# Another order of loads, and of everything behind them, in a fused attention and gating kernel

## The chip, the cores and the metric

The kernel runs on one core of a Trainium2 chip. The time is that of one execution on the device in microseconds (us), and less is better. Three runs of the kernel before gave 409.8, 411.2 and 410.75 us, with a median of 410.75 us.

## The reference, cut to what matters

There are 8 batches of 576 tokens, with 8 heads of 64 columns and 32 memory slots for each head. All data are float32.

```python
# for each batch and head
a   = softmax(phi, over the tokens)               # 576 x 32
k_m = a.T @ k ;  v_m = a.T @ v                    # 32 x 64 each
x   = softmax(q @ k_m.T / 8, over the slots) @ v_m   # the heads side by side: 576 x 512
# for each batch
h    = relu(x @ w_in)                             # 576 x 1024
u, v = h[:, :512], h[:, 512:]
v    = (v - mean(v)) / sqrt(var(v) + 1e-6)        # over the 512 columns
out  = (u * (w_spatial @ v + b_spatial)) @ w_out  # w_spatial is 576 x 576
```

## The kernel before, in words

The program is one long list of steps, written out by hand. Every kind of work is a generator; a letter in a list runs that generator up to its next `yield`, which is usually one instruction group on one engine. The three lists are `START` (lines 26 to 38: the weights, batch 0 and the beginnings of batches 1 and 2), `PLAN` (lines 40 to 47: repeated for batches 1 to 6) and `LAST` (lines 49 to 53: the end of batch 7). A digit after a letter picks a piece of the work (a block of tokens, of columns or of weights), each `'` means one batch ahead, and `*2` means twice. Each engine carries out its own instructions in the order in which the lists emit them, so a list fixes the queue of every engine, the load queue of SyncE (SP) among them. An instruction at the head of a queue that waits holds up everything behind it.

The letters that the texts below speak of are these.

- `P` (`memory_weights`, line 304) loads phi of a batch into the one buffer `phi_sb`, takes the softmax over tokens there, and sums it (`es`). The next phi can only be loaded when the `kvm` products have read the buffer.
- `K` (`memories`, line 337) loads k and then v into the one buffer `kv_sb`; the products `kvm` (line 351) need both; `den`, `kmn` and `vmn` divide by the sums, `tk` and `tv` turn them, and `kT` and `vT` are the copies of that.
- `Q` (`queries`) loads q. For batch 0 it is turned on TensorE (`tq`, copied to `qT_all` on ScalarE); for later batches it comes in pieces of 128 bytes and VectorE turns it (`qT`, line 445).
- `S` (`scores`, and `scores_first` for batch 0) multiplies q with the memories (`sc`), takes the softmax over slots (`rmx`, `sm`, `rsum`) and leaves it turned, as a high and a low part (`ah` and `al`).
- `D1` and `D0` (`load_win`) load the right and the left half of the columns of w_in, four pieces of 512 KB each. `E0` and `E1` decode the right half from the first and the last two pieces, `L0` and `L1` the left one. A decode has four instructions: ScalarE line 196, VectorE line 198 (the sign), ScalarE line 202, VectorE line 204 (the result, in `win_sb`).
- `M1` and `M0` (`products`) multiply the memories with the right and the left half of w_in (`mp`), again split into `mh` and `ml`.
- `V` (`gate`, five blocks of tokens: `pv`, the statistics `st` and `mv`, then `vh` and `vl`, for the last block the tile `t`) and `U` (`units`, four blocks of columns: `pu`, `u`) are the two halves of h.
- `W` (`load_spatial`) loads w_spatial (`w_sb`, 1152 KB, and `w_rem`) and the bias; `T0` to `T4` turn it on TensorE (`wt`) and split it into `wth` and `wtl`, and `B` puts the bias beside it.
- `G` (`spatial`, `ps`, `g`, `gh`, `gl`) multiplies with w_spatial and gates, `X` loads and decodes w_out, and `O` (`project`, `po`, `o`) multiplies with it and stores.
- `Z` (`warm_up`, line 798) is a product whose result nobody reads.

The low part of a split comes from one of two engines (`low`, line 156). If the name of the tile stands in `ON_VECTOR`, VectorE subtracts the high part (line 177). If it doesn't, TensorE subtracts it with one or two products (line 165) and ScalarE copies the rest (line 175). Names are `wtl` with the block, and `ml` with batch, half and part.

PSUM has two tags. `b1` has four buffers of one bank and `b2` has two buffers of two banks. The tiles of `T`, `U` and `G` and the scores are in `b2`, so a third of them waits until one of the two before it has been read for the last time.

In `START` before, SP loads in this order: phi, q, k and v of batch 0, the four pieces of `D1`, the first piece of `D0`, phi of batch 1, w_spatial, the rest of `D0`, k of batch 1, the first half of its q, its v, and the second half of its q.

Of the kernel before, what the change touches and what calls it, by code (L numbers as in the profile page):

```python
# [23 lines left out]


START = """
    P Q P Z P K*2 D1 P Q P*2 Q*2 P*2 Q P*3 Q P Z P Q D1 Q K E0 D1*2 P*2 K*2 Z K*2 E0 K Q*2 K E1
    K*2 E0 Q D0 E1*2 K P' E0 Z S P'*2 S W S P' S Z S D0 Z P' T0 T2 S T0 P' S*2 D0 E1 T0 T2 D0 P'
    S*2 P' S B S M1 P' L0 T0 T2 T1 M1 T2 S L1 S P' M1 S M1 L0 M1 S L1 S*4 T3 K' M1 S T1 L1 S Q' M1
    Z L0 L1 V2 L0 V2 V0 K' T1 P' V2 M0 P'*2 V0 M0 P' K' M0 P' V2 V0*2 M0 T1 K' M0 T4 Q' X1 T3 V1  # L30
    M0 V2 V0 M0 U2 K' V2 T3 U2 P'' V1 X1 T4 T3 V3 V0 U1 Q'*2 K' V1 X0 T4 X0 S U2 U1 K' T4 V1 K' U3
    K'*2 B U3 V2 V1 U1 V0 V1 U0*2 Q'*2 P'' V1 V3 K' X1 V3 U3 P'' V4 P'' V3 U0 X1 K' S' V4 S'*2 X0
    K'' M1' Q'' M0' M1' G0 S'*2 M1' V3 V4 K'' V3 G1 S' M1' G1 V4 P'' G1 V4 M0' G0 M0' V3 P'' G0
    V4*2 X0 P'' V4 G1 X1 P'' X0 S' G1 M0' X0 X1 G0 X0 M1' G3 G0 X0 M1' X1 P'' G3 X1 G1 G3 M0' G1
    G3 G0 G2 G1 G0 G2 P'' M0' G0 Q'' G1 M0' G0 G2*2 G3 O2 G2 O3 S' G2 S' G3 G2 P'' G3 O1 S' O3
    S'*2 O2 G2 S' O2 O3 S' P'' S' P'' O1 O0*2 O1 S' G2 P'' O1 S' G3 M1' G3 U2' S'*2 O3 O0*2 P''
    V1' Q'' O2 V1'*2 Q'' V1'
"""

PLAN = """  # L40
    K' V4 V0 U2 V1 P'' U0 V4 Q' U0 Q'' K' U1 K' Q' U1 V0 P'' V2 U3*2 V0 V3 V0 V2 K' U3 K' S' U1 S'
    K' M1' M0' V2 S'*2 V3 M1' V2 V3*2 V4 G0 V2 G1 S' V3 G0 S' M1' V3 V2 V4 V3 G1 V4 G1 S' M0'
    P''*2 M0' G1 S' G0*2 G3 G1 M1' M0' P'' Q'' G3 G0 G1 P'' S' G3 M0' M1' G1 G3 P'' M1' P'' M0'
    K'' S' G1 M1' G2*2 G0 G2 G1 G0 S' G0 O3 S' P'' G2 G0 O1 G3 G2 G3 S' G2 G3 G2 S'*2 O0 M0' S' O1
    U2' P'' O0 O3 O1 G3 P'' S'*2 P'' S' O0 O3 P''*2 O3 K''*2 V1' K'' O1 V4' V1' G3 V1' V4' O2*2
    V4' O0 V1' O2 P''' G2 V0'*2 G2 O4 Q'' V1' U2' O4 U0' V0' O4 V1' V2' K''' Q'' O2 O4 K''
"""

LAST = """
    U2 V0 V2 V0 V4 V0 U0 V1 U3 U0 U3 V3 V2 U1 V0 U3 V4 U1 V3 V2 G0 V4 U1 V2*2 V4 V3 G0 G1*2 V3 V2  # L50
    V3 V4 G1 G0 V3*2 G0*2 G1 G3 G0 G1 G3 G1 G2 G3 G2 G0 G2 G1*2 O2 G1 G2 O0 G2 G3 G2 V1 G2 G0 G2*2
    G3*3 O1*3 G3 O2 O0 O2 G0 O4 O1 G3 O4 O0 O4 O0 O4 O3*3 O2 O3
"""

FINAL = int(LAST.split()[-1][1])

ON_VECTOR = set(
    """
    E0 E1 L0 L1 X0 X0.sign X1 X1.sign ml000 ml001 ml010 ml101 ml110 ml111 wtl3 wtl4
""".split()  # L60
)

# [816 lines left out]
```

## Time and profile before

| what | value |
|---|---|
| median of three runs | 410.75 us |
| time of the profiled execution | 410.63 us |
| its span, from the first to the last instruction | 408.8 us |
| TensorE busy with products | 392.5 us (96%) |
| VectorE, ScalarE, GpSimd busy | 287.9, 229.9, 47.6 us |
| mean granted clock of TensorE | 0.994 of full |
| moved by the DMA engines | 50.7 MB |

In the rows further down PE is TensorE, DVE is VectorE, ACT is ScalarE and SPq is the queue of SyncE. A row of a timeline begins with its start and its length in us. Where the engine had been idle before it, the idle time and what ended it stand in brackets. Rows with `x2` hold two instructions in a row.

### The profile page before, as it was taken

The page shows a single profiled execution, that of the slowest core. Times are in us where ns is not written, and L with a number is a line of the kernel's source. Part 1 is how long each engine was busy: PE and PEld are TensorE (multiplying, and loading weights), DVE is VectorE, ACT ScalarE, POOL GpSimd, SP SyncE. Part 2 cuts the span into 40 slices and gives each one's busy share as a digit, 9 for nine tenths or more (in the row PEclk, how much of TensorE's full clock was granted, in tenths as well). Part 3 has the DMA queues.
Part 4 walks back from the last instruction along what each step waited for, and adds up shares of the span by engine and source line. Part 5 has one row for each costly group of instructions (what it writes and reads, how often), then busy time and mean ns, then how long its engine had stood idle before and what let it go on. Part 6 is the DMA issues. An engine that isn't in the chain of part 4 may idle for free.

```text
span 408.8 us, 9476 instructions
## 1 busy us (share of the span) xinstructions
PE 392.5 (96%) x3961; PEld 335.0 (82%) x3961; DVE 287.9 (70%) x543; ACT 229.9 (56%) x423; POOL 47.6 (12%) x131
## 2 busy tenths in 40 slices
PE   4788999999999999999999999999999999999996
PEld 2544779889898879989798879989798879989984
DVE  1589999986896469947796469947796559843430
ACT  2669888538634477247634477238635477148321
POOL 1000311002200310002200311002200311014000
PEclk9989999999999999999999999999999999999999
DMA  8999997023911683046801683045800210020003
GB/s 308 392 371 225 253 249 171 2 104 83 259 66 58 223 140 120 0 134 184 195 2 49 230 139 120 0 140 174 199 2 26 80 28 0 2 77 27 0 22 108
DMA packets 85790, 50.70 MB, mean 124 GB/s; under 512 B 66226, under 2 KB 70322, under 8 KB 85748
## 3 DMA queue, kind: packets, MB, share of 16 engines
q1 hardware_dynamic: 85748, 50.10, 43.0%
q8 instruction: 31, 0.51, 0.5%
q14 instruction: 11, 0.09, 0.1%
HBM read 40.65 MB, written 9.44 MB: 123 GB/s over the span
## 4 chain that ended last, share of the span: by engine, by line
PE 88%; DMA 5%; DVE 4%; ACT 1%; issue 1%; SPq 0%; ACTq 0%
PE ps L734 29%; PE po L774 24%; PE pu L696 12%; PE pv L630 10%; PE kvm L351 4%; PE mp L598 3%; DMA kv_sb<-in_v_dram 3%; DMA w_sb<-in_moe_w_spatial_dram 2%; PE sc L532 2%; PE pv L639 1%; PE pv L640 1%; ACT raw L202 1%; PE wt L264 0%; DVE ml L177 0%; PE tk L391 0%
## 5 line engine op out<-in xcount | busy, mean ns | idle before, releaser
L734 PE MATMUL ps<-wth,vh 128*128 128x288 f32 x256 | 56.3, 301 | 0.0
L734 PE MATMUL ps<-wth,vl 128*128 128x288 f32 x256 | 54.8, 295 | 0.0
L734 PE MATMUL ps<-wtl,vh 128*128 128x288 f32 x256 | 54.5, 294 | 0.0
L756 ACT CAST gh<-g 128x512 fp32r<-128x512 f32 x32 | 19.7, 620 | 56.2 <-DVE g L745 55.9
L774 PE MATMUL po<-woh,gl 128*128 128x512 f32 x128 | 50.4, 393 | 0.0
L774 PE MATMUL po<-woh,gh 128*128 128x512 f32 x128 | 50.2, 392 | 0.0
L774 PE MATMUL po<-wol,gh 128*128 128x512 f32 x128 | 50.2, 392 | 0.0
L659 POOL TENSOR_SCALAR rs<-mv 128x1 f32<-128x1 f32 (+1 forms) x40 | 9.2, 229 | 322.1 <-DVE mv L656 313.6
L734 PEld LDWEIGHTS ps<-wth,vh 128*128 128x128 f32 x256 | 41.1, 188 | 6.6 <-PE mp L598 5.9
L654 DVE BATCH_NORM_STATS2 st<-vr 128x6 f32<-128x512 f32 (+1 forms) x40 | 27.3, 683 | 21.8 <-ACT vr L635 16.9
L734 PEld LDWEIGHTS ps<-wth,vl 128*128 128x128 f32 x256 | 41.1, 188 | 0.0
L734 PEld LDWEIGHTS ps<-wtl,vh 128*128 128x128 f32 x256 | 41.0, 188 | 0.0
L784 ACT COPY o<-po 128x512 f32<-128x512 f32 x35 | 20.4, 587 | 34.0 <-PE po L774 34.0
L674 DVE TENSOR_TENSOR vl<-vr,vh 128x512 fp32r<-128x512 f32 x32 | 21.9, 687 | 24.1 <-ACT vh L672 24.0
L669 ACT ACTIVATE vr<-vr,sh,rs 128x512 f32<-128x512 f32 (+1 forms) x40 | 32.7, 816 | 0.3 <-POOL sh L664 0.2
L635 ACT ACTIVATE vr<-pv 128x512 f32<-128x512 f32 x32 | 19.2, 600 | 23.2 <-PE pv L630 23.0
L745 DVE TENSOR_TENSOR g<-u,ps 128x576 f32<-128x576 f32 x32 | 23.9, 749 | 10.5 <-PE ps L734 10.5
L774 PEld LDWEIGHTS po<-woh,gh 128*128 128x128 f32 x128 | 24.0, 188 | 5.6 <-ACT vr L635 1.2
L774 PEld LDWEIGHTS po<-woh,gl 128*128 128x128 f32 x128 | 24.0, 188 | 5.3
L696 PE MATMUL pu<-ah,mh 128*128 128x288 f32 x128 | 27.8, 299 | 0.5 <-DVE qT L445 0.5
L774 PEld LDWEIGHTS po<-wol,gh 128*128 128x128 f32 x128 | 24.1, 188 | 4.4
L696 PE MATMUL pu<-al,mh 128*128 128x288 f32 x128 | 27.5, 296 | 0.0
(143 smaller groups left out, 855.0 us busy)
## 6 DMA issues: line engine op xcount, KB each, us to landing
kv_sb<-in_k_dram SPq DMA_DIRECT2D x8, 1152.0 KB, 8.2
kv_sb<-in_v_dram SPq DMA_DIRECT2D x8, 1152.0 KB, 8.1
out_dram<-o SPq DMA_DIRECT2D x32, 256.0 KB, 2.7
q_sb<-in_q_dram SPq DMA_DIRECT2D x28, 288.0 KB, 4.8
phi_sb<-in_phi_dram SPq DMA_DIRECT2D x8, 576.0 KB, 5.2
raw<-in_moe_w_in_dram SPq DMA_DIRECT2D x8, 512.0 KB, 11.4
raw<-in_moe_w_out_dram SPq DMA_DIRECT2D x4, 512.0 KB, 6.6
q_all<-in_q_dram SPq DMA_DIRECT2D x1, 1152.0 KB, 6.5
```

The source lines that it names most:

```text
L351: nc.tensor.matmul(kvm[r][32 * j : 32 * j + 32], phi_sb[halves[r], j, i, :], kv_sb[halves[r], j, :, i * D : (i + 1) * D], start=(i == 0), ...
L630: nc.tensor.matmul(pv, x[:, r, cs], m[:, r, DM:DFF], start=(n == 0), stop=(n == 5))
L635: nc.scalar.activation(vr, pv, AF.Relu)
L654: nc.vector.bn_stats(st6, vr)
L669: nc.scalar.activation(vr, vr, AF.Identity, bias=sh, scale=rs)
L674: nc.vector.tensor_tensor(vl[:, st, :], vr, vh[:, st, :].bitcast(F32), op=ALU.subtract)
L696: nc.tensor.matmul(pu[:, hf, 0:HALF], m[:, r, cs], a[:, r, hf * HALF : (hf + 1) * HALF], start=(n == 0), stop=(n == 5),)
L734: nc.tensor.matmul(ps[:, hf, 0:HALF], a, w[:, hf * HALF : (hf + 1) * HALF], start=(n == 0), stop=(n == len(ops) - 1),)
L745: nc.vector.tensor_tensor(g.rearrange("p (a s) -> p a s", a=2), u[:, dt, :].rearrange("p (a s) -> p a s", a=2), ps[:, :, 0:HALF], op=ALU.mult,
L756: nc.scalar.copy(hi, x)
L774: nc.tensor.matmul(po, a, w, start=(n == 0), stop=(n == 11))
L784: nc.scalar.copy(o, po)
```

## The change

Only the three lists and the set `ON_VECTOR` change. The generators are the same, and every step of them still runs. SP's new order at the start is: phi and q of batch 0, the first piece of `D1`, k, the second piece of `D1`, v, the last two pieces of `D1`, w_spatial and the bias, phi of batch 1, the four pieces of `D0`, the first half of q of batch 1, its k, its v, and the second half of its q. On ScalarE the first instructions of both decodes `E0` and `E1` stand ahead of `kmn`, and there is one product `Z` less. `wtl1` and `ml100` move to VectorE, and `ml010` and `ml111` leave it. The order of all other work, in the batches behind as in the first, is new.

```diff
--- before.py
+++ after.py
@@ -24,39 +24,38 @@
 
 
 START = """
-    P Q P Z P K*2 D1 P Q P*2 Q*2 P*2 Q P*3 Q P Z P Q D1 Q K E0 D1*2 P*2 K*2 Z K*2 E0 K Q*2 K E1
-    K*2 E0 Q D0 E1*2 K P' E0 Z S P'*2 S W S P' S Z S D0 Z P' T0 T2 S T0 P' S*2 D0 E1 T0 T2 D0 P'
-    S*2 P' S B S M1 P' L0 T0 T2 T1 M1 T2 S L1 S P' M1 S M1 L0 M1 S L1 S*4 T3 K' M1 S T1 L1 S Q' M1
-    Z L0 L1 V2 L0 V2 V0 K' T1 P' V2 M0 P'*2 V0 M0 P' K' M0 P' V2 V0*2 M0 T1 K' M0 T4 Q' X1 T3 V1
-    M0 V2 V0 M0 U2 K' V2 T3 U2 P'' V1 X1 T4 T3 V3 V0 U1 Q'*2 K' V1 X0 T4 X0 S U2 U1 K' T4 V1 K' U3
-    K'*2 B U3 V2 V1 U1 V0 V1 U0*2 Q'*2 P'' V1 V3 K' X1 V3 U3 P'' V4 P'' V3 U0 X1 K' S' V4 S'*2 X0
-    K'' M1' Q'' M0' M1' G0 S'*2 M1' V3 V4 K'' V3 G1 S' M1' G1 V4 P'' G1 V4 M0' G0 M0' V3 P'' G0
-    V4*2 X0 P'' V4 G1 X1 P'' X0 S' G1 M0' X0 X1 G0 X0 M1' G3 G0 X0 M1' X1 P'' G3 X1 G1 G3 M0' G1
-    G3 G0 G2 G1 G0 G2 P'' M0' G0 Q'' G1 M0' G0 G2*2 G3 O2 G2 O3 S' G2 S' G3 G2 P'' G3 O1 S' O3
-    S'*2 O2 G2 S' O2 O3 S' P'' S' P'' O1 O0*2 O1 S' G2 P'' O1 S' G3 M1' G3 U2' S'*2 O3 O0*2 P''
-    V1' Q'' O2 V1'*2 Q'' V1'
+    P*4 Q Z P*2 Q D1 Q K P*3 Q D1 P*2 Q P*2 Q*3 K P*2 Q K D1 E0 D1 K E1 K Z Q K*5 W K E1 S E1 Q P'
+    S T0 E0 T0 E1 K S D0 S E0 D0 B S*2 T0 D0 P' S Z D0 S T2 Q' E0 T0 T2 L0 P' Z S P' M1 K' S K' T2
+    P' Z S M1 T2 P' Q' P' T3 S M1 L1 L0 P' S M1 S P' M1 S P' T3 S T1 S*4 M1 S M1 Z S L1 P' V0 P' B
+    T1 L1 V2 L0 L1 T3 L0 V0 K' P' M0 T1*2 V2 P' V0 P' K' M0 T4 M0 V2 X1 M0 V0 V1 M0 K' T4 T3 X1 V2
+    K'*2 T4 M0 V0 M0 V2 P'' X0 V1 K' T4 U0 Q' U0 U1*2 K' V2 Q' K' V1 K'' X1 U0 V3 V2 U2 V0 U2 U1
+    U3 Q' S V1 V3 V1 K' X1 P'' V0 V3 U3 V4 K' Q' V3 P'' S' V1 M1' M0' U2 G0 U3 X0 P'' V1 P'' Q''
+    V4 S'*2 M1' V3 V4 G0 X0 V4 X1 V4 V3 S'*2 V4 G1 P'' M0' M1' V4 G1 M1' S' M0' X0 K'' P''*2 G0 V3
+    V4 X0 G1 G0 X1 M1' G0 G1 M1' G2 X0 G1 M0' X1 X0 S' G0 G1 G2 P''*2 X0 G3 X1 G3*2 G0 G2 G1 G3 G2
+    G1 O2 O3 G0 S' G1 G0 M1' G2*2 G3 M0' G3 G2 S' M0' P'' G3 S' O1 O2 O3 O1 S' Q'' O0 O2 S'*3 P''
+    S' O3 O0 S' O3 G2 S' G3 O2 S'*2 O1 G3 V1' G2 O0 P'' V1' M0' P''*2 O0 O1
 """
 
 PLAN = """
-    K' V4 V0 U2 V1 P'' U0 V4 Q' U0 Q'' K' U1 K' Q' U1 V0 P'' V2 U3*2 V0 V3 V0 V2 K' U3 K' S' U1 S'
-    K' M1' M0' V2 S'*2 V3 M1' V2 V3*2 V4 G0 V2 G1 S' V3 G0 S' M1' V3 V2 V4 V3 G1 V4 G1 S' M0'
-    P''*2 M0' G1 S' G0*2 G3 G1 M1' M0' P'' Q'' G3 G0 G1 P'' S' G3 M0' M1' G1 G3 P'' M1' P'' M0'
-    K'' S' G1 M1' G2*2 G0 G2 G1 G0 S' G0 O3 S' P'' G2 G0 O1 G3 G2 G3 S' G2 G3 G2 S'*2 O0 M0' S' O1
-    U2' P'' O0 O3 O1 G3 P'' S'*2 P'' S' O0 O3 P''*2 O3 K''*2 V1' K'' O1 V4' V1' G3 V1' V4' O2*2
-    V4' O0 V1' O2 P''' G2 V0'*2 G2 O4 Q'' V1' U2' O4 U0' V0' O4 V1' V2' K''' Q'' O2 O4 K''
+    U0 V1 Q' K' V0 U2 V4 V1 K' V0*2 P'' V2 Q' V0 U3 U1*2 V3 P'' K' V2*2 K' U3 U1 V4 S' P'' S' K'
+    S' V3 S' V4 V2 V3 S' M1' V4*2 V2 M0' S' G0*2 M0' V3 M1' V3 P'' V3 V2 V3 G1*2 S' G0 M1' G1 S'
+    G0 G1 P'' M1' G0 M1' G2 G0 G2 M0' G1 P''*2 S' G3 G0 P'' G2 G1 G0 S' P'' S' G1 M1' G3*3 G1 M1'
+    G2 O1 G1 G0 G3 G2 S' G2 G3 S' G2 S' G3 P'' O0 S' M0' S' O1 M0' O0 O1 G3 P'' U0' U2' P'' O3 M0'
+    G2 S' O0 O3 P'' G2 S' M0' P'' K''*2 G3 O4 S' O3 V0' Q'' O4 V1' V4' O2 O1 V0' Q'' K'' U2' P'''
+    O3 O2 O4 O0 U0' Q''' V1' Q'' K'' K''' V1'*2 O4 V4' V1' V0' K''' V2' V4' O2*2 K'' U3'
 """
 
 LAST = """
-    U2 V0 V2 V0 V4 V0 U0 V1 U3 U0 U3 V3 V2 U1 V0 U3 V4 U1 V3 V2 G0 V4 U1 V2*2 V4 V3 G0 G1*2 V3 V2
-    V3 V4 G1 G0 V3*2 G0*2 G1 G3 G0 G1 G3 G1 G2 G3 G2 G0 G2 G1*2 O2 G1 G2 O0 G2 G3 G2 V1 G2 G0 G2*2
-    G3*3 O1*3 G3 O2 O0 O2 G0 O4 O1 G3 O4 O0 O4 O0 O4 O3*3 O2 O3
+    V1 V0 U0 V3 V0 V2 U2 U3 V0 V4 V1 V4 U1 V2 V0 V3 U3 V4 U1 V2 V3*2 V2 U1 V2 G1 V4 V3 G1 G0 V2 G0
+    V3 V4 G0 V3 G1*3 G0 G1 G0 G2*3 G0*2 G1 G2 G1 G3 G0*2 G3 O1 G2 G3*2 G1 G3 O4 G3 G2 G3 O3 G3 G2
+    G3 O3 G2 O3 G2 O2 U3 O0 U0 O3 O1 O4 O2 O0 O1 O4 O1 O2 O4 O2 O0*2
 """
 
 FINAL = int(LAST.split()[-1][1])
 
 ON_VECTOR = set(
     """
-    E0 E1 L0 L1 X0 X0.sign X1 X1.sign ml000 ml001 ml010 ml101 ml110 ml111 wtl3 wtl4
+    E0 E1 L0 L1 X0 X0.sign X1 X1.sign ml000 ml001 ml100 ml101 ml110 wtl1 wtl3 wtl4
 """.split()
 )
 
```

## Rows read from the trace of the kernel before

**Rows 1.** The page, DMA share in 40 slices of the span, in tenths.
```profile
DMA  8999997023911683046801683045800210020003
```

**Rows 2.** Waits of PE, whole run: who waited for whom, us, times, longest.
```profile
PE wt L264 <- DMA w_sb<-in_moe_w_spatial_dram: 1.4, 1, 1.4
...
PE pu L696 <- DVE qT L445: 0.5, 1, 0.5
```

**Rows 3.** Busy time by engine, 30 to 80 us; then clock and DMA.
```profile
30.00:80.00 50.00, 47.72 (x505) 38.50 (x490) 48.16 (x77) 41.23 (x67) 6.61 (x16) 0.98 0.76 189
```

**Rows 4.** Timeline of SP's queue, the load of w_spatial.
```profile
16.59 0.51 SPq L248 DMA_DIRECT2D w_sb<-in_moe_w_spatial_dram  x1
```

**Rows 5.** Timeline of ACT, 16 to 20 us.
```profile
16.24 1.12 ACT L196 ACTIVATE raw<-raw 128x1024 int32<-128x1024 uint32 x1 [2.92 <-DMA raw<-in_moe_w_in_dram]
17.27 0.61 ACT L378 ACTIVATE kmn<-kvm,den 128x128 f32<-128x128 f32 x2
...
18.77 1.14 ACT L196 ACTIVATE raw<-raw 128x1024 int32<-128x1024 uint32 x1
19.82 0.35 ACT L400 COPY kT<-tk 128x256 f32<-128x256 f32 x1
```

**Rows 6.** Timeline of PE, 13 to 61 us.
```profile
13.84 2.22 PE L351 MATMUL kvm<-kv_sb,phi_sb 64*32 64x128 f32 x143 [1.21 <-DMA kv_sb<-in_v_dram]
...
21.16 2.07 PE L463 MATMUL sc<-kT,qT_all 64*64 64x32 f32 x116 [0.28 <-issue]
...
41.67 0.43 PE L165 MATMUL wt<-wth,minus 128*128 128x256 f32 x2
42.03 1.09 PE L598 MATMUL mp<-win_sb,vT 64*32 64x512 f32 x16
42.91 2.21 PE L351 MATMUL kvm<-kv_sb,phi_sb 64*32 64x128 f32 x143
...
45.13 1.09 PE L264 MATMUL wt<-ident,w_sb 128*128 128x128 f32 x8
...
48.57 0.42 PE L696 MATMUL pu<-ah,mh 128*128 128x288 f32 x2 [0.50 <-DVE qT L445]
...
60.52 0.54 PE L734 MATMUL ps<-wth,vh 128*128 128x288 f32 x2
```

**Rows 7.** Timeline of DVE, 22 to 66 us.
```profile
22.73 0.69 DVE L295 TENSOR_TENSOR half<-phi_sb 128x512 f32<-128x512 f32 x1 [0.21 <-DMA phi_sb<-in_phi_dram]
...
23.79 0.82 DVE L477 TENSOR_REDUCE rmx_all<-sc 128x20 f32<-128x640 f32 x1
...
29.04 0.29 DVE L317 TENSOR_REDUCE cm<-mt 128x2 f32<-128x128 f32 x1 [0.84 <-PE mt L314]
...
33.94 0.69 DVE L177 TENSOR_TENSOR ml<-mp,mh 128x512 fp32r<-128x512 f32 x1
...
36.43 1.22 DVE L198 SCALAR_TENSOR_TENSOR raw<-raw 128x1024 int32<-128x1024 int32 x1
37.56 1.65 DVE L514 TENSOR_TENSOR al<-ta,ah 128x384 fp32r<-128x384 f32 x2
39.12 2.50 DVE L204 SCALAR_TENSOR_TENSOR win_sb<-raw 128x1024 int32<-128x1024 int32 x2
...
46.38 0.74 DVE L177 TENSOR_TENSOR wtl<-wt,wth 128x576 fp32r<-128x576 f32 x1
...
50.42 0.76 DVE L287 TENSOR_TENSOR ws<-b_sb,ws 1x576 fp32r<-1x576 f32 x1
...
58.39 0.68 DVE L650 TENSOR_TENSOR vr<-vr,pv 64x512 f32<-64x512 f32 x1 [0.51 <-ACT vr L649]
...
65.46 0.69 DVE L682 TENSOR_TENSOR t<-vr,t 64x512 fp32r<-64x512 f32 x1
```

**Rows 8.** Busy by engine, granted clock, DMA, in two single microseconds.
```profile
25.00:26.00 1.00, 0.14 (x1) 0.00 (x0) 1.00 (x3) 0.42 (x1) 0.00 (x0) 1.00 0.98 303
...
29.00:30.00 1.00, 1.00 (x11) 0.36 (x17) 0.96 (x2) 0.83 (x3) 0.00 (x0) 0.50 1.04 395
```

## The prediction

> **What bounds the kernel now.** I read first who waited for whom on TensorE, because it is busy for 96% of the span. Its waits end early: the last one that the profile names is `pu` at 48.57 us [rows 2, 6]. From there to the end TensorE has no gap that ends in a wait, so batches 1 to 7 cost what their products cost, and a new order of them can only add gaps. What the change can win lies ahead of 48.57 us. Two things are full there. The DMA engines are busy in nine tenths or more of every slice of 10.2 us from the second to the sixth [rows 1], so a load that goes first makes another one late. And VectorE is busy for 48.16 of the 50 us from 30 to 80 [rows 3], so a step that VectorE gets later stays later.
>
> **The loads.** Before, the first decode on ScalarE waits for the second piece of w_in and starts at 16.24; six transfers are then in: phi, q, k, v and two pieces [rows 5]. After, v is the last of the same six. With the DMA engines full I take the same landing, 16.24, so `kvm` starts 2.4 us later than its 13.84 [rows 6], at 16.25. The decode of the second pair of pieces starts at 18.77 before [rows 5], and the same eight transfers are ahead of that in both orders, so 18.77 stays.
>
> W_spatial is issued at 16.59 before, behind phi of batch 1, which has to wait until `kvm` has read its buffer [rows 4]. After, nothing holds it, and it lands before the scores end. The 1.4 us that `wt` waits for it [rows 2] go. They bring little: what is late next is the chain from v through the scores to `al`, on which `pv` hangs.
>
> **The chain of batch 0.** In the new order of ScalarE both first decodes stand ahead of `kmn`. The second starts at 18.77 and takes 1.05 us to the next start (18.77 to 19.82), so `kmn` starts at 19.85, where the sums of `kvm` would let it start at 17.27 + 2.4 = 19.7. Before, from `kmn` at 17.27 to the end of `sc` at 21.16 + 2.07 = 23.23 are 5.96 us, and the second decode is in them with its 1.05 [rows 5, 6]. After it is not, so `sc` ends at 19.85 + 4.9 = 24.75, and `rmx` starts at 24.85. Before it starts at 23.79, held half a us by the two steps of phi's maximum in front of it.
>
> From `rmx` to the end of `al`, VectorE takes 23.79 to 37.56 + 1.65 = 39.21, 15.42 us [rows 7]. The new order takes out one sign step of w_in (36.43 to 37.56, 1.13) and one `ml` (0.69), and brings in the two steps of phi's maximum that were ahead of `rmx` (22.73 to 23.79, 1.06). One decode result stands in it in both. The idle 0.84 ahead of `cm` may go too, or a new wait may take its place: 13.8 us without and 14.7 with it. So `al` ends between 38.65 and 39.5; I take 38.9, near the lower end, as `cm` now has other work in front of it. That is 0.3 earlier than before, and the two loads ahead of v have eaten the rest.
>
> **Behind it.** What was taken out of VectorE's queue ahead of `al` now stands behind it, in front of the left half of w_in, and `M0` needs that. After `al` come a sign step (1.13), a step of phi's sum (0.69, as the same form in [rows 7]), the bias row (0.76) and two decode results (2.43 to the next start): 5.0 us, so `mp` of `M0` can start at 43.9. Before it started at 42.03. TensorE ends two `pv` groups at 41.4 and the half of `kvm` that is moved ahead (1.1 of the 2.22 from 42.91 to 45.13) at 42.5, and then waits 1.4 us. From 43.9 it has `mp` (0.88), the other half of `kvm` (1.1), then `wt` of the last block and a `pv` (2.94 from 45.13 to the wait at 48.07): 48.8 [rows 6].
>
> There `pu` needs one of the two PSUM buffers of tag `b2`. Its last reader is `wtl3` on VectorE (46.38 to 47.12 before). From the end of the decode results (41.62) to there are 5.5 us before; after, one phi step (0.69) and one `ml` (0.6) are out and `wtl1` (0.74) is in: 4.95, so 48.85. `pu` would start at 49.0, 0.4 later than 48.57. Moving `wtl1` to VectorE saves the 0.36 us of its product on TensorE (41.67 to 42.03); the wait hides that saving.
>
> The next tie is the tile `t` of the last `gate` block, which ends at 65.46 + 0.69 = 66.15 before, 19.0 us behind `wtl3` [rows 7]. After, one `ml` (0.6) comes in, the bias row (0.76) is out, and the idle 0.51 ahead of `vr` goes, as VectorE is late: 18.4, so 67.25. The last part of the first `ps` group needs it. Six parts of 0.8 us and 0.8 us of the seventh, 5.6 us, lie between the first `ps` and that; `ps` may then start no earlier than 61.65 without a gap, against 60.52 before: 1.1 late. TensorE alone is 0.4 late, VectorE alone 1.1; I take 0.9, nearer to VectorE, as it is the engine without idle time.
>
> **The rest at nothing.** One product `Z` fewer is off the chain. `ml010` becomes a product and a copy ahead of `pv`, where TensorE waits anyway, and `ml111` changes places with `ml100`. Between 100 and 340 us the same products run, with waits on VectorE and ScalarE between them but none on TensorE; I put the new order there at nothing, with 0 and 6 times 0.5 us (the wait of `pu` in [rows 2], once in each of six batches) as its ends. `LAST` ends as before in one last `po`, its copy in two halves and its store.
>
> **Sum.** 410.63 of the profiled execution (span 408.8 and 1.8 around it) plus 0.9 is 411.5. That execution lies 0.1 below the median of the three runs, so I predict 411.5 as the median too, 0.2% above 410.75. The measurement can't tell less than 0.3%, 1.2 us, from no change. The forecast's own range is 410.4 to 412.4.
>
> **Rivals.**
>
> *VectorE is no limit, and TensorE runs through.* My sum makes VectorE late by adding single steps, and an error of 1 us in it is easy. If no wait takes the place of the old ones, `pu` starts when the work in front of it ends: 48.57, less the wait of 0.5, the 0.36 of `wtl1`'s product and the 0.3 by which `al` is early, is 47.4. That gives 410.63 - 1.15 = 409.5; with the lower end for `al` 409.2, and with v landing earlier than its place in the sum as low as 408.4. For it speaks that no wait is left on TensorE behind 48.57 though VectorE is as full there; against it, the 5.0 us of VectorE work that the new order puts between `al` and `M0`. Chance 0.32.
>
> *`pu` waits longer for its buffer.* Before, `wtl3` ends at 47.12 and TensorE is there at 48.07, yet `pu` starts at 48.57, with a `qT` transposition two steps further on VectorE named as its releaser [rows 2, 6, 7]. If the same lag of 1.45 us behind `wtl3` holds, `pu` starts at 48.85 + 1.45 = 50.3, 1.7 late, and 0.9 to 1.7 is added to what VectorE already costs: 412.3 to 413.3. It decides as soon as `wtl3` ends later than 47.9. Chance 0.12.
>
> *The later batches get gaps.* One wait of 0.5 us in each of six batches makes 411.5 + 3 = 414.5, half of that 413. The trace of before shows no wait there, and VectorE is far less full than in the start. Chance 0.10.
>
> *TensorE's clock falls in the new wait.* At 25 to 26 us TensorE is busy for 0.14 us; at 29 to 30 the granted clock is 0.50, 1.2 instead of 2.4 GHz, though it is busy throughout [rows 8]. If the wait in front of `M0` does the same, the 4.9 us from `mp` to `pu` take up to twice as long; for 1 to 4.9 us at half the clock 0.5 to 4.9 us are lost, and I take 1.5: 413. Against it, the stretch ahead of 42.5 holds two full `pv` groups. Chance 0.06.
>
> The Trainium skill (TensorE: Matmul & The Clock Gate, "What's actually happening") says that the array's clock is gated to half when it has been idle, and is given back only after lasting activity. The trace agrees in rows 8. By that rule this rival would be the forecast if 1.4 us of waiting were idle enough, which no row shows.
>
> **How the numbers follow.** The forecast has 0.40, of which 0.32 is within 0.3% and 0.08 above. The first rival gives 0.24 faster and 0.08 within. The second gives 0.01 within and 0.11 slower, the third 0.01 and 0.09, the fourth 0.01 and 0.05. So faster 0.24, within 0.3% 0.43, slower 0.33. The range from 408.6 to 413.5 leaves out the far end of the first rival and those of the last two.
>
> **What would show it.** Right: `kvm` at 16.2 and `kmn` at 19.9; no wait for w_spatial; `mp` of `M0` behind a wait of 1 us or more for a decode result; `pu` at 49 to 49.5; the first `ps` group at 61 to 62; TensorE without waits from 100 us on. Wrong: `kvm` before 15.5 or a first `pv` before 37.5, which would make it faster than I say, and any wait of TensorE behind 90 us, which would make it slower.

## The result, and the profile after

The changed kernel takes 415.61 us (median of four runs, 414.9 to 416.32), and the kernel before beside it 410.34. The ratio is 1.0127, with a 95% interval from 1.0105 to 1.0148. I had said 411.5 and a range that ends at 413.5, so the prediction was wrong: the change makes the kernel slower, and by more than the range allowed.

The profiled execution of the changed kernel took 414.9 us with a span of 413.1, 4.3 us more than the 408.8 of before; the medians are 5.3 apart, and what the other 1.0 is these two profiles don't show. Two marks on TensorE split that. The first `sc` of batch 1 starts at 60.61 instead of 57.67, so the start loses 2.9 us. From there to the start of the last `po` are 348.1 us instead of 346.8, so the batches behind lose another 1.3, although TensorE waits for nothing there in either kernel.

TensorE's waits after, in the view of who waited for whom (us in total, times, longest), which answers to [rows 2]:

```profile
PE kvm L350 <- DMA kv_sb<-in_v_dram: 4.1, 1, 4.1
...
PE kvm L350 <- ACT vr L634: 1.8, 1, 1.8
```

The wait for w_spatial and that of `pu` are gone, as they were meant to be. The wait of `kvm` for v, 1.21 us before, is now 4.1. The timeline of TensorE, which answers to [rows 6], shows what stood ahead of it and what followed:

```profile
9.95 2.77 PE L418 MATMUL tq<-ident,q_all 128*128 128x128 f32 x12
16.81 4.09 PE L350 MATMUL kvm<-kv_sb,phi_sb 64*32 64x128 f32 x144 [4.09 <-DMA kv_sb<-in_v_dram]
...
24.33 2.05 PE L462 MATMUL sc<-kT,qT_all 64*64 64x32 f32 x112 [0.22 <-issue]
...
45.50 1.35 PE L350 MATMUL kvm<-kv_sb,phi_sb 64*32 64x128 f32 x79 [1.78 <-ACT vr L634]
...
46.63 1.10 PE L597 MATMUL mp<-win_sb,vT 64*32 64x512 f32 x15
...
48.59 1.09 PE L263 MATMUL wt<-ident,w_sb 128*128 128x128 f32 x8
...
51.39 0.42 PE L695 MATMUL pu<-ah,mh 128*128 128x288 f32 x2
...
60.61 1.20 PE L531 MATMUL sc<-qT,kT 64*32 64x288 f32 x32
...
63.45 0.53 PE L733 MATMUL ps<-wth,vh 128*128 128x288 f32 x2
```

The same 144 products of `kvm` that took 2.22 us before take 4.09, nearly twice as long. The windows (stretch, its length, busy time and number of instructions by engine, then granted clock, DMA share, GB/s) show 48 of them in a microsecond:

```profile
17.00:18.00 1.00, 1.00 (x48) 1.00 (x45) 0.00 (x0) 0.00 (x0) 0.00 (x0) 1.00 1.00 406
```

The clock column reads 1.00 there, but the first record that this profile has of the clock is its rise at 21.2 us, and ahead of the first record the column reads 1.00 in every run. In two kernels below it reads 0.50, 1.2 instead of 2.4 GHz, over the same products at the same pace (51 and 53 in a microsecond). In the kernel before, where `kvm` takes 2.22 us, there are 95:

```profile
15.00:16.00 1.00, 1.00 (x95) 1.00 (x78) 0.00 (x0) 0.00 (x0) 0.00 (x0) 1.00 1.05 389
```

So I read half clock from the pace here. The pace says one thing more. In the kernel before, the products `tq` that turn q go from slow to fast ahead of `kvm`; the two products of a `Z` run between these rows:

```profile
10.05 1.06 PE L419 MATMUL tq<-ident,q_all 128*128 128x128 f32 x4
...
12.02 0.60 PE L419 MATMUL tq<-ident,q_all 128*128 128x128 f32 x4
```

In the changed kernel this `Z` isn't ahead of `kvm`, and all twelve `tq` up to 12.7 us go at the slow pace. So two things can have `kvm` at half clock: the standstill of 4.09 us, and a clock that hadn't risen when it began. The next link is ScalarE's, which answers to [rows 5]:

```profile
14.07 1.13 ACT L195 ACTIVATE raw<-raw 128x1024 int32<-128x1024 uint32 x1
19.33 1.14 ACT L195 ACTIVATE raw<-raw 128x1024 int32<-128x1024 uint32 x1 [4.14 <-DMA raw<-in_moe_w_in_dram]
21.66 0.62 ACT L377 ACTIVATE kmn<-kvm,den 128x128 f32<-128x128 f32 x2 [1.19 <-DVE den L373]
...
42.27 2.19 ACT L201 ACTIVATE raw<-raw 128x1024 f32<-128x1024 f32 x2
44.31 1.10 ACT L634 ACTIVATE vr<-pv 128x512 f32<-128x512 f32 x2
```

The second decode ends at 20.5 and `kmn` still waits 1.19 us, for the sums of `kvm`. The last two rows are the other new wait: the relus of `pv` stand behind two decode steps on ScalarE, and `kvm` of batch 1 waits 1.78 us for the PSUM buffers that they free. They end at 45.41. The load of v of batch 1, issued at 34.67, lands at 45.37, so without the relus the wait would have been as long. In a profile of the same start with the old lists behind it (below) the load ends this wait:

```profile
45.45 1.37 PE L350 MATMUL kvm<-kv_sb,phi_sb 64*32 64x128 f32 x80 [2.26 <-DMA kv_sb<-in_v_dram]
```

VectorE, answering to [rows 7]:

```profile
26.42 0.82 DVE L476 TENSOR_REDUCE rmx_all<-sc 128x20 f32<-128x640 f32 x1 [0.71 <-PE sc L462]
...
35.04 0.29 DVE L316 TENSOR_REDUCE cm<-mt 128x2 f32<-128x128 f32 x1 [1.09 <-PE mt L313]
...
38.58 2.52 DVE L513 TENSOR_TENSOR al<-ta,ah 128x384 fp32r<-128x384 f32 x3
...
43.65 2.36 DVE L203 SCALAR_TENSOR_TENSOR win_sb<-raw 128x1024 int32<-128x1024 int32 x2
```

So `al` ends at 41.10 instead of 39.21, and the decode results that `M0` needs at 46.0.

### The profile page after: what moved, and what is told of

It is laid out like the page before. It is cut to its first block, busy times and chain, and to the rows that moved or that the text cites. A ratio compares the mean times of both kernels' runs of the same rounds, so it can differ in the third digit from the quotient of the medians.

```text
span 413.1 us, 9469 instructions
## 1 busy us (share of the span) xinstructions
PE 394.8 (96%) x3958; PEld 337.5 (82%) x3958; DVE 285.4 (69%) x543; ACT 228.7 (55%) x423; POOL 51.3 (12%) x131
## 4 chain that ended last, share of the span: by engine, by line
PE 92%; DMA 3%; DVE 2%; ACT 1%; SPq 1%; issue 0%; ACTq 0%
PE ps L733 29%; PE po L773 25%; PE pu L695 12%; PE pv L629 10%; PE kvm L350 5%; PE mp L597 3%; DMA kv_sb<-in_v_dram 3%; PE sc L531 2%; PE idle L797 1%; PE pv L639 1%; PE pv L638 1%; PE wt L263 1%; PE sc L462 1%; DVE raw L197 1%; ACT raw L201 1%; PE tk L390 0%
## 5 line engine op out<-in xcount | busy, mean ns | idle before, releaser
L783 ACT COPY o<-po 128x512 f32<-128x512 f32 x35 | 20.5, 586 | 38.5 <-PE po L773 38.5
L634 ACT ACTIVATE vr<-pv 128x512 f32<-128x512 f32 x32 | 19.1, 600 | 26.9 <-PE pv L629 26.5
```

Source lines behind the costliest of these rows:

```text
L634: nc.scalar.activation(vr, pv, AF.Relu)
L783: nc.scalar.copy(o, po)
```

## Experiments on the start

My theory after this: v behind two pieces of w_in costs the start nearly everything, by the later landing (3.0 us) and because TensorE stands still for 4 us and then runs `kvm` at half its clock (1.9 us). The rivals were the rest of the new order of the start, and the new plan of the later batches.

**Warming TensorE.** Three products `Z` stand in the wait for v.

```diff
-    ... P*2 Q*3 K P*2 Q K D1 E0 D1 K E1 K Z Q K*5 W K E1 ...
+    ... P*2 Q*3 K P*2 Q Z*3 K D1 E0 D1 K E1 K Z Q K*5 W K E1 ...
```

> Three products that nobody reads stand on TensorE between the turning of q and kvm of batch 0. Theory (the array's clock): kvm takes 4.1 us after the change instead of 2.2 because TensorE had been idle for 4.1 us and runs at half its clock. Then kvm comes back to about 2.2 us, kmn starts near 19.9 to 20.2 instead of 21.66, al ends 1 to 1.8 us earlier, and the time falls by 1 to 2 us from the changed kernel, to 413.5 to 414.6. Rival (kvm is slowed by the loads that write SBUF meanwhile, or by its late operand): kvm stays at 4 us and the time within 0.5 us of the changed kernel's 415.6.

Measured: 417.14 us, ratio 1.0163 (1.0140 to 1.0186). TensorE's timeline and two microseconds of the windows:

```profile
17.07 2.22 PE L350 MATMUL kvm<-kv_sb,phi_sb 64*32 64x128 f32 x143 [1.62 <-DMA kv_sb<-in_v_dram]
...
24.53 2.11 PE L462 MATMUL sc<-kT,qT_all 64*64 64x32 f32 x118 [1.47 <-issue]
```

```profile
27.00:28.00 1.00, 0.98 (x5) 0.47 (x3) 0.97 (x2) 0.00 (x0) 0.00 (x0) 0.50 1.02 406
32.00:33.00 1.00, 1.00 (x3) 0.68 (x3) 1.00 (x1) 0.94 (x3) 0.00 (x0) 0.50 0.55 86
```

`kvm` is back at 2.22 us, with v as late and the DMA engines as full, so the clock was what slowed it, as the theory said. Whether the standstill or the missing `Z` had left it at half, this run can't tell. The time isn't back, and there the theory failed: `sc` then stops for 1.47 us for which the profile shows no releaser, and the clock is at half from 26.6 to 33.4 us, twice as long as in the changed kernel (28.1 to 31.5).

**v first.** v is loaded ahead of both pieces; the rest is the changed kernel.

```diff
-    P*4 Q Z P*2 Q D1 Q K P*3 Q D1 P*2 Q P*2 Q*3 K P*2 Q K D1 ...
+    P*4 Q Z P*2 Q Q K P*3 Q K P*2 Q P*2 Q*3 D1*2 P*2 Q K D1 ...
```

> Of the change only the place of the two w_in pieces is undone: SP loads k and v of batch 0 ahead of all four pieces; w_spatial still goes ahead of phi of batch 1. Theory (the pieces ahead of v cost v's delay and with it the clock): kvm starts at 13.9, takes 2.2 us, and kmn starts behind the second decode at about 19.9, so al ends 1.5 to 2 us earlier than in the changed kernel and the time is 413.3 to 414.3. Rival (the start is limited by VectorE's order behind al, whatever the loads do): within 0.5 us of 415.6.

Measured: 412.9 us, 1.0074 (1.0046 to 1.0102), and the first `sc` of batch 1 at 57.49, where it was before. So the place of v among the loads is worth the whole loss of the start. It is so although `kvm`, which I had expected at 2.2 us, still takes 4.09. (From there to the last `po` it has 349.2 us, more than either kernel; that is taken up with the later batches.)

```profile
14.17 4.09 PE L350 MATMUL kvm<-kv_sb,phi_sb 64*32 64x128 f32 x144 [1.09 <-ACT qT_all L420]
```

`kvm` is slow here too, behind a wait of only 1.09 us; the kernel before had 1.21 us, and a `Z` between the transpositions of q. So here it isn't the standstill: all twelve `tq` go at the slow pace here too, and the first record of the clock is its rise at 19.0, behind `kvm`. I put that `Z` back (`Q*3` becomes `Q Z Q*2`):

> The changed kernel with v loaded ahead of the two pieces of w_in, and one product Z between the transpositions of q as in the kernel before (the run with v first had none there, and its kvm took 4.1 us after a wait of 1.1). Theory (TensorE's half clock in kvm comes from too little work ahead of it): kvm starts at 14.2 and takes 2.2 us, kmn then waits for the second decode on ScalarE, so the first sc of batch 1 comes at 55.8 to 57.0 (57.5 with v first alone), and the time is 411.2 to 412.6 (412.9 with v first alone; gh and vh both stand at odd multiples of 32 bytes here too). Rival (the Z only lengthens the queue ahead of kvm, or the slow clock comes later instead, as in the run with three Z): 57.5 or later and 412.9 to 414.

Measured: 417.05 us, 1.0151 (1.0127 to 1.0174), far off the theory, and past the 414 of the rival. The timeline and the windows:

```profile
14.43 2.76 PE L350 MATMUL kvm<-kv_sb,phi_sb 64*32 64x128 f32 x144
...
20.82 0.44 PE L390 MATMUL tk<-ident,kmn 128*128 128x128 f32 x2 [2.10 <-ACT vmn L386]
...
21.72 4.00 PE L462 MATMUL sc<-kT,qT_all 64*64 64x32 f32 x144 [0.35 <-ACT kT L399]
```

```profile
23.00:24.00 1.00, 1.00 (x48) 1.00 (x48) 1.00 (x1) 0.21 (x1) 0.00 (x0) 0.50 1.14 368
28.00:29.00 1.00, 1.00 (x3) 0.76 (x4) 1.00 (x3) 0.98 (x2) 0.00 (x0) 0.50 1.04 345
```

`kvm` gained 1.3 us, and TensorE then waited 2.1 us for `kmn` and `vmn`, which stand behind the second decode on ScalarE, as my prediction had it for the changed kernel. The clock went to half from 22.3 to 32.6 us, most of `sc` included. The next run takes that wait away too, by putting the decode behind `kmn`, `vmn` and `kT`:

```diff
-    ... K D1 E0 D1 K E1 K Z Q K*5 W K E1 S E1 Q P'
+    ... K D1 E0 D1 K K Z Q K*5 W K E1*2 S E1 Q P'
```

> The changed kernel with v ahead of the two pieces, one Z between the transpositions of q, and the second decode of w_in on ScalarE moved behind kmn, vmn and kT. With the decode ahead of kmn TensorE waited 2.1 us for vmn (v first and Z), and the clock was at half from 22.3 to 32.6 us: 417.05. Theory (the waits of the start cost more by the half clock behind them than by their length): kmn at 17.4, tk at 18.6 without a wait over 1 us, sc in 2.1 to 2.6 us, first sc of batch 1 at 55.5 to 57.0; with po at 233 to 234 ns 410.8 to 412.3. Rival (the half clock comes anyway, in another place; or the later batches take back what the start gains): 413 or more.

Measured: 415.63 us, 1.0119 (1.0094 to 1.0144): the rival. `kvm` took 2.22 us and `tk` started at 18.23, but `sc`, which began at 19.13, was stopped twice (0.85 us without a named releaser and 0.81 for `qT_all`), the clock was at half from 22.9 to 29.8, and the first `sc` of batch 1 came at 58.78. So with v first the `Z` alone takes `kvm` from 4.09 to 2.22 us, and the time rose all the same: what the 1.9 us of `kvm` are worth by themselves, these runs don't show.

**Each part alone, in the kernel before.** First the two pieces of w_in (`P Q P Z P K*2 D1` becomes `P Q P Z P D1 K D1 K`, and one later `D1` goes):

> The kernel before with one edit: two pieces of w_in are loaded earlier, one between q and k, one between k and v of batch 0; no tile changes its place. Theory (v behind two pieces of w_in is the loss of the start): kvm starts at 16.0 to 17.1 instead of 13.84 and takes 3.7 to 4.1 us instead of 2.2, the first sc of batch 1 comes at 60 to 61 instead of 57.7, and with po at 229 ns the time is 413.0 (412.4 to 414.0). Rival (the loss of the start needs the rest of the new order, such as both first decodes ahead of kmn and kvm of batch 1 in halves): sc at 57.7 to 59 and 410.4 to 411.8.

Measured: 413.66 us, 1.0068 (1.0046 to 1.0091).

```profile
16.85 3.60 PE L351 MATMUL kvm<-kv_sb,phi_sb 64*32 64x128 f32 x144 [3.53 <-DMA kv_sb<-in_v_dram]
...
31.16 0.38 PE L264 MATMUL wt<-ident,w_sb 128*128 128x128 f32 x2 [1.55 <-issue]
...
60.78 1.20 PE L532 MATMUL sc<-qT,kT 64*32 64x288 f32 x32
```

```profile
18.00:19.00 1.00, 1.00 (x51) 1.00 (x43) 0.00 (x0) 0.00 (x0) 0.00 (x0) 0.50 1.03 414
```

This is the theory: `kvm` starts at 16.85, and the start loses 3.1 us, as much as the whole change. The `Z` is in its old place here, the clock is at full from 12.8 us on and falls at 16.3, in the standstill, and the column reads 0.50 over most of `kvm`. So here it is the standstill that has `kvm` at half clock. Then w_spatial ahead of phi of batch 1 (`K P' E0 Z S P'*2 S W S` becomes `K W P' E0 Z S P'*2 S S`):

> The kernel before with one edit: w_spatial and the bias are loaded ahead of phi of batch 1. The products po keep their 229 ns, since no tile changes its place. Theory (the loss comes from v behind two pieces of w_in): this part costs nothing; the wait of wt for w_spatial (1.4 us) goes, VectorE's chain decides, first sc of batch 1 at 57.2 to 57.9 and 409.9 to 410.8. Rival (phi of batch 1, 0.9 us or more later, and the pieces of w_in behind it cost): sc at 58.5 or later and 411.3 or more.

Measured: 413.23 us, 1.0059 (1.0038 to 1.0079): the rival. First a row of TensorE, then three of VectorE:

```profile
29.88 1.09 PE L264 MATMUL wt<-ident,w_sb 128*128 128x128 f32 x4 [4.00 <-DVE sm_all L479]
```

```profile
26.92 0.69 DVE L295 TENSOR_TENSOR half<-phi_sb 128x512 f32<-128x512 f32 x1 [4.32 <-DMA phi_sb<-in_phi_dram]
27.64 0.42 DVE L297 TENSOR_TENSOR half<-half 128x256 f32<-128x256 f32 x1
27.99 0.82 DVE L477 TENSOR_REDUCE rmx_all<-sc 128x20 f32<-128x640 f32 x1
```

With the order of before on VectorE, the two steps of phi's maximum stand ahead of `rmx`. Phi lands 4.2 us later (its step starts at 26.92 instead of 22.73), `rmx` waits with it, and `wt` waits for a PSUM buffer of the scores. The first `sc` of batch 1 comes at 60.23, 2.6 us late. In the changed kernel these steps stand behind `rmx`, so this price isn't paid there: the parts cost 2.6 and 3.1 us alone and 2.9 together. That the new order of VectorE makes the early w_spatial free follows from this comparison alone; no run has that order by itself.

**Filling the wait of the kernel before.** Three more `Z` at 25 to 26.5 us (`S D0 Z P' T0` becomes `S D0 Z*4 P' T0`):

> The kernel before with three more products Z in the wait of TensorE for w_spatial at 25 to 26.5 us. Before, TensorE stands still there for 1.4 us, and the granted clock is 0.50 from 28.5 to 31.9 us. Theory (the stretch at half follows the standstill, and it is paid for in the chain behind): no stretch at 0.50 behind 20 us, the first sc of batch 1 at 56.0 to 57.2 and 409.2 to 410.0. Rival (the stretch comes anyway, later or longer, as with Z in the changed kernel, or VectorE's chain hides it): 57.4 or later and 410.3 to 411.5.

Measured: 412.68 us, 1.0059 (1.0041 to 1.0077): the way of the rival, and past its range. One of the `Z` waits for `sm_all`, `wt` starts at 28.24 instead of 26.55, and the half clock is 6.8 us long and comes at 34.6 instead of 28.5. None of the four tries to take a standstill out of the start beat the kernel that it set out from: 417.1 against 415.6 for the changed kernel, 417.05 and 415.63 against 412.9 for v first, 412.68 against 410.35 for the kernel before. That the later stretch at half clock is what they lost isn't shown. Its place differs between runs of the same instructions: in the kernel before it lies at 28.5 to 31.9 us, and with other places of its tiles (below) at 33.2 to 40.0, with the first `sc` of batch 1 no later (57.31).

## Experiments on the later batches

**Which list.** The new `START` with the old `PLAN` and `LAST` (with the steps that these need from it):

```diff
-    ... O1 G3 V1' G2 O0 P'' V1' M0' P''*2 O0 O1
+    ... O1 G3 U2' V1' G2 O0 P'' V1' M0' P''*2 O0 O1 Q'' V1'*2 Q''
```

> The new START (with one pu part of batch 1 and four steps at its end, that the old plan expects there) with the PLAN and LAST of the kernel before. Theory (two losses: 2.9 us up to the first scores of batch 1, and 1.3 to 1.4 us spread over the later batches and the end): 413.2 to 413.9. Rival (all of it comes from the start, and the later batches only follow): 415 to 416.

Measured: 415.0 us, 1.0121 (1.0096 to 1.0147), and 347.9 us from the first `sc` of batch 1 to the last `po`: the rival, all of the loss with the old plan. Here the clock column covers `kvm` (first the windows, then its row):

```profile
17.00:18.00 1.00, 0.95 (x40) 0.98 (x48) 0.00 (x0) 0.00 (x0) 0.00 (x0) 0.50 1.02 414
18.00:19.00 1.00, 1.00 (x53) 1.00 (x43) 0.00 (x0) 0.00 (x0) 0.00 (x0) 0.50 1.01 393
```

```profile
17.05 3.72 PE L350 MATMUL kvm<-kv_sb,phi_sb 64*32 64x128 f32 x144 [4.17 <-DMA kv_sb<-in_v_dram]
```

The Trainium skill (TensorE: Matmul & The Clock Gate, "What's actually happening") says that TensorE's clock is at half by default and that activity releases it; the rows agree, 0.50 behind 4.17 us without a product. In this run of the new start the clock had risen, at 13.4 us, in the standstill, and fell at 16.8, just ahead of `kvm`; in the profile of the changed kernel it has no rise ahead of 21.2. `kvm` is at half clock in both. The counterpart is the old `START` with the new `PLAN` and `LAST`:

> The START of the kernel before with the new PLAN and LAST. Theory (two losses): 1.0 to 1.6 us above the kernel before, 411.4 to 412.0. Rival (all from the start): within 0.4 us of the kernel before, 410.0 to 410.8.

Measured: 410.86 us, 1.0011 (0.9995 to 1.0027), and 346.5 us. So the new plan is worth nothing that shows, against my theory, and the 1.3 us of the later batches come with the start.

What a start can leave behind to batch 7 isn't an order of work. The products themselves are slower: the groups of `po` in the page after, whose means were 392, 392 and 393 ns before:

```profile
L773 PE MATMUL po<-woh,gh 128*128 128x512 f32 x128 | 50.9, 397 | 0.0
L773 PE MATMUL po<-wol,gh 128*128 128x512 f32 x128 | 50.8, 397 | 0.0
L773 PE MATMUL po<-woh,gl 128*128 128x512 f32 x128 | 50.6, 396 | 0.0
```

From one start to the next it is 234 ns instead of 229 (medians over the 432 `po` products), 1.8 us in all; the other products give about half a us of it back. A tile gets its place in SBUF when it is first named, so a new `START` gives the tiles other places. `gh`, the weights of most `po`, moved from byte 123200 of each partition to 137696. I first tried `gh` alone, with 32 bytes of padding ahead of it and behind it:

```diff
+        if tag == "gh":
+            one.tile([P, 8], F32, name="pad0")
         raw = one.tile([P, 2, 2 * 512], I32, tag=tag, name="raw")
+        if tag == "gh":
+            one.tile([P, 8], F32, name="pad1")
```

> The changed kernel, with 32 bytes of unused SBUF put ahead of the tile gh and 32 behind it; no instruction differs. A tile gets its place in SBUF when it is first named, so the new START moves gh from byte 123200 of each partition (a multiple of 64) to 137696 (32 more than one); here it stands at 137728, a multiple of 64 again, and gl, vh and vl stand as they stood to 64. In the traces the products po follow each other behind 68 us every 229 ns (median) in before and in the old START with the new plan, and every 233 to 234 ns in every kernel with the new START. Theory (the place of gh, the weights of po, sets that pace): po back at 229 to 230 ns, 432 products by 4.1 ns = 1.8 us less, so 413.8 (412.8 to 414.3) instead of 415.6; the start unchanged, the first sc of batch 1 at 60.6. Rival (the pace follows from the order of instructions or from the PSUM buffers of po): 233 to 234 ns and 415 to 416.3 as before.

Measured: 414.35 us, 1.0093 (1.0059 to 1.0127), `po` at 232 ns, 347.2 us between the marks instead of 348.1. Its six runs lie apart (three at 412.9, three from 415.8 to 417.0), so the marks say more than the median. The same pads in the kernel before:

> The kernel before, with the same two pads of 32 bytes around gh; no instruction differs. gh moves from a multiple of 64 bytes to 32 more than one (123232). Theory (the place of gh): po at 233 to 234 ns instead of 229 and 1.8 us more, 412.1 (411.5 to 412.8). Rival (order or PSUM buffers): 229 ns and 410.4.

Measured: 411.26 us, 1.0014 (1.0002 to 1.0026), `po` at 231 ns, 347.6 us instead of 346.8. Both go the way of the theory, by half of what it said. With four small tiles made larger, so that all weight tiles stand at multiples of 64 bytes:

> The kernel before, with four small tiles (cm, den, rmx, rsum) made larger so that gh, gl, vh, vl, u and all behind them stand at multiples of 64 bytes; gl, vl and u don't in the kernel before. Theory (the place of a weight tile sets the pace of its products): the po with gl as weights and the one ahead of it, 229 and 231 ns before, come to 226 as the one with gh; 144 of each kind, (3 + 5) ns by 144 = 1.2 us less, and up to 0.3 from ps with vl: 409.0 (408.5 to 409.6). Rival (only the place of gh matters, or none): 410.4.

Measured: 410.57 us, 1.0003 (0.9989 to 1.0016), `po` at 231 ns and 347.1 us. The rule of 64 bytes is wrong: `po` got slower. In the kernels with v first `vh`, the weights of two thirds of `ps`, has moved as well, and `ps` follow each other every 133 ns instead of 132. The kernel with `kmn` first, with pads around both `gh` and `vh`:

> As the run with kmn first, with pads of 32 bytes around vh and gh, which then stand at multiples of 64 bytes. Theory (the place of gh and vh is worth what it was in the changed kernel, 0.9 us of the sum of po, and ps 132 instead of 133 ns in median, 0.5 to 0.9 in sum): po 231 to 232 ns and 1.2 to 1.8 us less than kmn first alone, 409.4 to 410.8, so no slower than the kernel before. Rival (the place makes no difference here): the same as kmn first alone.

Measured: 414.1 us, 1.0080 (1.0056 to 1.0105), 347.45 us instead of 349.3, so 1.9 less between the marks, with `po` at 232 and `ps` at 132 ns. The median fell by 1.5, within the 1.2 to 1.8 that I had said; 409.4 to 410.8 was missed, as `kmn` first itself took 415.63. In the profile its start was 1.4 us later (first `sc` of batch 1 at 60.21).

To have places and order apart, each kernel then got all places of the other: every tile is named once, unused, at the head of the program, and no instruction changes.

```diff
+    for tag, n in PLACES:
+        one.tile([P, n], F32, tag=tag, name="place")
```

> The kernel before, instruction for instruction, but with the tiles named once, unused, at the head of the program in the sequence of the changed kernel, so that every tile stands at the byte of SBUF at which it stands in the changed kernel. Theory (what the batches behind the first lose goes with the places of the tiles, not with the order of the work): from the first sc of batch 1 to the start of the last po 347.9 to 348.3 us instead of 346.8, po at 233 to 234 ns, and 411.7 (411.3 to 412.3). Rival (the order of the start sets it, through PSUM or what its loads leave behind): 346.8, po at 229 ns, 410.5.

> The changed kernel, instruction for instruction, with every tile at the byte of SBUF at which it stands in the kernel before. Theory (places): 346.5 to 347.0 us from the first sc of batch 1 to the start of the last po instead of 348.1, po at 229 ns, and 414.3 (413.4 to 415.0); what is left to the kernel before, 3.0 to 3.9 us, is the start. Rival: 348.1, 234 ns, 415.6.

Measured: the kernel before with the places of the changed one 411.8 us, 1.0035 (1.0022 to 1.0047), 348.2 us between the marks; the changed kernel with the places of before 413.35 us, 1.0075 (1.0056 to 1.0094), 346.2 us. Their groups of `po` in the page, first the kernel before with the new places, then the changed kernel with the old ones:

```profile
L778 PE MATMUL po<-wol,gh 128*128 128x512 f32 x128 | 50.8, 397 | 0.0
L778 PE MATMUL po<-woh,gh 128*128 128x512 f32 x128 | 50.7, 396 | 0.0
L778 PE MATMUL po<-woh,gl 128*128 128x512 f32 x128 | 50.7, 396 | 0.0
```

```profile
L777 PE MATMUL po<-woh,gl 128*128 128x512 f32 x128 | 50.4, 394 | 0.0
L777 PE MATMUL po<-woh,gh 128*128 128x512 f32 x128 | 50.3, 393 | 0.0
L777 PE MATMUL po<-wol,gh 128*128 128x512 f32 x128 | 50.2, 392 | 0.0
```

The pace goes with the places, in both directions. That settles the 1.3 us: the places of the tiles, not the order of the work, make the later batches slower. The changed kernel gained 2.3 us in its median, 0.8 more than the kernel before lost; 0.5 of that lies between the marks (1.9 against 1.4 us), and where the rest comes from the profile doesn't show, as its start was no faster (61.44).

The loss of the start goes with the order. In the five profiles with the old `START`, whatever its plan or the places of its tiles, the first `sc` of batch 1 comes at 57.3 to 58.2 us; in the four with the new one, at 60.6 to 62.5.

| kernel | median, us | first `sc` of batch 1 | from there to the last `po` |
|---|---|---|---|
| before | 410.3 to 410.8 | 57.67 | 346.8 |
| before, two pieces of w_in ahead | 413.66 | 60.78 | 346.9 |
| before, places of after | 411.8 | 57.31 | 348.2 |
| after, places of before | 413.35 | 61.44 | 346.2 |
| after | 415.61 | 60.61 | 348.1 |

## Why the prediction was wrong

**The step that failed** is "so `kvm` starts 2.4 us later than its 13.84, at 16.25", and what it took as given: that `kvm` then takes its 2.22 us. I moved the landing and kept the length. It started at 16.81, 0.6 later than said, and took 4.09, 1.9 more, so it ended 2.4 us later than in my sum. I had the mechanism among the rivals, but put it in front of `M0`, at 0.06, where I expected a new wait. I didn't ask the same of the wait that was largest in my own sum, the one of `kvm` for v: at 16.25 the sum gave it 1.21 + 2.4 = 3.6 us of standstill, and [rows 8] had shown the clock at half behind one of 1.4 us.

A second term had the same end. "One product `Z` fewer is off the chain" was put at nothing, but this `Z` ran ahead of `kvm`: with v first, `kvm` took 4.09 us without it and 2.22 with it. Each of the two had `kvm` at half clock in a run without the other (the standstill, with the `Z`, made 3.60), and the changed kernel has both. The two loads ahead alone, in the kernel before, lost 3.1 us of the start, and v first gave them back. How much of that is the landing and how much the clock stays open, since the runs that gave `kvm` its full clock lost time elsewhere.

**The second decode ahead of `kmn`** was no limit. It started at 19.33 (said: 18.77), `kmn` at 21.66 (said: 19.85) behind `den`. With v first it was one: TensorE waited 1.0 us for it, and 2.1 with the `Z`.

**The chain to `al`.** From the start of `rmx` to the end of `al` it is 14.7 us, the upper end of my 13.8 to 14.7. `rmx` started 1.6 late and `al` ended at 41.10 against 38.9, 2.2 late, so most of that was there before VectorE had begun.

**`M0` and `pu`.** I said `mp` at 43.9 behind a decode result; it came at 46.6, and TensorE's wait in front of it was another one, 1.78 us for relus that ScalarE had behind its decode steps and, as late, for v of batch 1. I had followed the buffers of `b2` and neither those of `b1` nor that load. The decode results came at 46.0. From the end of `al` to the first `sc` of batch 1 are 19.5 us instead of 18.5, near the 1.2 us that I had given this part, but from another wait: that is luck. `pu` came at 51.39 without the wait for its buffer that I gave it, since TensorE was later than VectorE.

**The wait for w_spatial** went, as said, and brought nothing that shows. That the late phi costs 2.6 us unless VectorE's order is changed with it was in no step of mine.

**The later batches "at nothing"** is right for the order (346.5 us with the new plan, 346.8 with the old) and wrong in the sum, by 1.3 us. The reason isn't in any rival: I had no term for the length of a product, and the places of the tiles change it.

**The rivals.** The first had TensorE run into `pu` without a wait; it did, but 2.8 us late. The second's longer wait for the buffer didn't come. The third, gaps in later batches, named 413 to 414.5, but no gap came. The fourth, the clock, was the right mechanism at the wrong place. The sum of 0.9 should have been 2.9 for the start and 1.3 behind it.

## What to carry to other kernels

When a load is put behind others, price the standstill of TensorE that it makes, and then the products behind it at half the clock, where the trace of before shows that a standstill does that; here they took 4.09 us instead of 2.22. A product that nobody reads isn't off the chain if the clock rises by it: look at the pace of the products behind it before it is taken out. Filling the standstill with idle products didn't pay here: `kvm` became fast, and all four kernels that tried to fill or to remove a standstill became slower. And when a program's order changes, compare the products' spacing in a stretch without waits; if it differs, look at where the tiles stand before looking at the order, and keep the places by naming the tiles in the old sequence.

## What the runs showed that I had not expected

The spacing of `po` moves by 2% (229 to 234 ns) with the SBUF places of tiles alone. Which place is good stays open: with 32 bytes of shift it went both ways, and multiples of 64 bytes are not the rule.

The profile names no releaser for several stops of TensorE in the start, of 0.85 to 1.8 us (`sc` or `wt`, "issue"), in the kernels with three `Z`, with `kmn` first (with and without pads) and with two pieces of w_in ahead. They came while the DMA engines were full (share 1.01 to 1.10 in these stretches); what TensorE waited for there wasn't tried.
